# First block's attention queued behind the second chunk's chain, attention later in the first four periods, second layer three tiles behind the first

## The chip, the cores and the metric

The kernel runs on one core of one Trainium2 chip. The time is device microseconds (us) of one execution, and the median of several executions counts; lower is better. A core has five engines with a queue of their own each: TensorE (PE; its weight loads are shown as PEld), VectorE (DVE), ScalarE (ACT), GpSimd (POOL) and SyncE (SP, which here only issues DMA transfers). Each engine works through its own instructions in the order in which the built program has them.

## The reference

Two stages. The first is a complex gated linear attention over 4 batches, 8 heads, 768 tokens and head size 48; its output, seen as 3072 tokens of 384 channels, goes through eight dense expert networks (384 to 1024 to 384) that are weighted by a gate with eight rounds of row and column normalisation.

```python
for t in range(S):
    new_re = ar * S_re - ai * S_im
    new_im = ar * S_im + ai * S_re
    S_re, S_im = new_re + kv, new_im          # kv = k[t] v[t]^T
    y[:, :, t] = einsum('bhd,bhde->bhe', q[:, :, t], S_re)
...
P = np.exp(logits)                            # logits = x @ w_gate, less their maximum
for _ in range(8):
    P /= P.sum(1, keepdims=True) + 1e-09
    P /= P.sum(0, keepdims=True) + 1e-09
    P *= N / E
for e in range(E):
    out += P[:, e:e + 1] * (np.maximum(x @ w1[e], 0.0) @ w2[e])
```

## The kernel before, in words

The 3072 tokens are cut into 12 **blocks** of 256, and each block into two **chunks** of 128. There are two phases.

Phase 1 makes the attention and, on the way, experts 0 and 1. For each block there are three pieces of work:

- The **chain** (`elem`, `chain`, `scan`): the gates a of the block (tile z) are normalised, multiplied up along the chunk by a scan of complex products on DVE (`cmul`: tiles cm_a, cm_b, or a, b in block 0), then turned into keys divided by the products (tile kh, L393) and queries times the products (tile z again, L400). ACT makes squares and reciprocal roots between (L362 to L368 at the start, L381 to L386 at the end). The results go to DRAM (kd, qd) and come back in another layout (ks, qs) before PE can use them. Block 0 runs its two chunks as two chains, one after the other, so that the first can start early.
- The **attention** (`mix`), a generator with five steps for each chunk, ten for a block: keys (transposes ktp, L438) and first scores (sp, L452); state (U, L447) and the other keys; outputs (y, L469) and second scores; state; outputs, the new state on DVE (L490 to L501) and the block's x as a pair of a rounded part xh (ACT, L503) and a rest xl (DVE, L504). Between scores and outputs DVE masks the scores (L455). ACT copies the chunk's last gate product out of qs (rr and rn, L419 to L421).
- The **experts** (`experts`): 16 tiles for a block (two experts, eight slices of 128 of the 1024). A tile is a first layer (ph, nine matmuls L176 to L178), a relu in two forms on ACT (hh, L182; hf, L183), a rest on DVE (hl, L184), and a second layer (po, six matmuls L155 to L157), which is issued LAG tiles later.

PE's order is written out by hand. In **period** i PE runs the 16 tiles of block i-1, and from tile number LEAD on one step of block i's attention after each tile; steps that are left at the end of the period follow without a tile between them. With LEAD = 4 the ten steps stand behind tiles 4 to 13. Block 0's attention runs before any tile, between the preparations of four of expert 1's weight slices (`load_w`: cast on ACT L123, difference on PE L127 and L128, copy on ACT L129); the other four slices are loaded in halves in period 1, one half behind each of its first eight tiles (`load_late`, L137 to L142). The orders on DVE, ACT and SP are made by a scheduler from the program's dependences and its own estimates of time; `issue_after(x)` makes it put what follows behind x on x's engine, without a wait.

Phase 2a (`phase2a`) runs the last block's remaining 14 tiles in small groups (`more(k)`), between the steps of the check, the softmax and the first normalisation rounds (`rows` on DVE, `columns` with one PE product cp, L573). Phase 2b runs experts 2 to 7 with matrix products of fewer multiplications; the remaining rounds stand in its first steps.

Of the kernel before, what the change touches and what calls it, by code (L numbers as in the profile page):

```python
# [18 lines left out]
CH = 128  # L19
# [3 lines left out]
SK = 112  # L23
N1 = 8
RING = 12
LAG = 2
LEAD = 4
TR = 4
TB = 32
UN = 768  # L30
# [1 line left out]
NS = UN // SUB  # L32
SU = 2
ITERS = 8
GT = 16


# [16 lines left out]
class Net:  # L54
# [132 lines left out]
    def phase1(self, c1, ca):  # L187
        tc, nc = self.tc, self.nc
        PS = bass.MemoryType.PSUM
        self.hp = c1.enter_context(tc.tile_pool(name="hp1", bufs=3))  # L190
        wx = c1.enter_context(tc.tile_pool(name="wx", bufs=NF + N1 - RING))
        self.xp = c1.enter_context(tc.tile_pool(name="xp1", bufs=2))
        self.psB = c1.enter_context(tc.tile_pool(name="psB", bufs=2, space=PS))
        self.fix = ca.enter_context(tc.tile_pool(name="fix", bufs=1, side="right"))
        self.ain = ca.enter_context(tc.tile_pool(name="ain", bufs=2, side="right"))
        self.tmp = ca.enter_context(tc.tile_pool(name="tmp", bufs=2, side="right"))
        self.psS = ca.enter_context(tc.tile_pool(name="psS", bufs=2, space=PS))
        self.psY = ca.enter_context(tc.tile_pool(name="psY", bufs=1, space=PS))
# [12 lines left out]
        self.ist = 0  # L211
        self.rr = [fix.tile([SK, H], F32, name=f"rr{i}") for i in range(2)]
        self.rn = [fix.tile([SK, H], F32, name=f"rn{i}") for i in range(2)]
        self.sb = fix.tile([SK, H, D], F32, name="sb")
        for t in self.rr + [self.sb]:
            nc.gpsimd.memset(t, 0.0)
        self.xs, self.vt, self.kqd = {}, {}, {}
        ns = self.N // SUB
        self.moe = self.experts()
        next(self.moe)  # L220
        self.elem(0, True)
        for f in range(NF):
            self.load_w(0, f, wx)
        late = [(1, f, j) for f in range(RING - NF, NF) for j in range(2)]

        for i in range(ns):
            mix = self.mix(i)
            if i == 0:
                for n, _ in enumerate(mix):
                    if n % 2 == 0 and n < 2 * (RING - NF):  # L230
                        with tc.issue_after(self.kd0.ins), tc.issue_after(self.sq0.ins):
                            self.load_w(1, n // 2, wx)
                with tc.issue_after(self.gl.ins):
                    self.elem(1)
                continue
            lg = self.logits(i - 1)
            for n in range(2 * NF):
                self.moe.send((i - 1, n // NF, n % NF))
                if n in (1, 2):
                    next(lg)  # L240
                if late:
                    self.load_late(*late.pop(0), wx)
                if n >= LEAD:
                    next(mix, None)
            for _ in mix:
                pass
# [100 lines left out]
    def chain(self, i, ns_, zt, qk, alloc):  # L347
# [30 lines left out]
        for j in range(CH, ZW):  # L378
            nc.scalar.activation(cut(zt[:, :, :, j:j + 1]), z[:, :, :, CH - 1:CH], AF.Copy)
        sq, x, g0 = alloc("sq"), alloc("x"), alloc("g0")  # L380
        sq_ = nc.scalar.activation(sq, z, AF.Square)  # L381
        V.scalar_tensor_tensor(x, sq[:, 0], 1e-26, sq[:, 1], ALU.max, ALU.add)
        o = 2 * ns + i * NCT * NCH + n0 * NCT
        nc.scalar.activation(fl[:, o:o + G], x[:, :, CH - 1], AF.Copy)
        nc.scalar.activation(g0, x, AF.Abs_reciprocal_sqrt)
        nc.scalar.activation(g0, g0, AF.Square)  # L386
        V.tensor_tensor(x, x, g0, ALU.mult)
        self.gl = V.scalar_tensor_tensor(g0, x, -2.0, g0, ALU.add, ALU.mult)
        V.scalar_tensor_tensor(x, g0, -1.0, qk[:, 1], ALU.mult, ALU.mult)
# [1 line left out]
        kd, qd = self.kqd[i]  # L391
        for a in range(2):
            V.tensor_tensor(kh[:, a], x, z[:, a], ALU.mult)  # L393
            dma = nc.sync.dma_start(
                kd[a, :, ns_].rearrange("(c p) n t -> p c (n t)", c=NCT),
                kh[:, a].rearrange("p (c n) t -> p c (n t)", c=NCT))
        if i == 0 and n0 == 0:
            self.kd0, self.sq0 = dma, sq_
        for a in range(2):
            V.tensor_tensor(z[:, a], z[:, a], qk[:, 0], ALU.mult)  # L400
            nc.sync.dma_start(
                qd[a, :, ns_].rearrange("(c p) n t -> p c (n t)", c=NCT),
                zt[:, a].rearrange("p (c n) t -> p c n t", n=NCH)[:, :, ns_].rearrange("p c n t -> p c (n t)"))

    def mix(self, i):
        nc, tmp = self.nc, self.tmp
# [5 lines left out]
        for c in range(NCH):  # L412
            ib = (i * NCH + c) % 2
            qs, ks, rr, rn = self.qs[ib], self.ks[ib], self.rr[ib], self.rn[ib]
            for a in range(2):
                nc.sync.dma_start(ks[64 * a:64 * a + D], kd[a, :, c].rearrange("(h d) t -> d h t", d=D))
                nc.sync.dma_start(qs[64 * a:64 * a + D], qd[a, :, c, :CH + 1].rearrange("(h d) t -> d h t", d=D))
            R = qs[:, :, CH]
            nc.scalar.activation(rr[0:D], R[0:D], AF.Copy)  # L419
            nc.scalar.activation(rr[64:64 + D], R[0:D], AF.Copy)  # L420
            nc.scalar.activation(rn[0:D], R[64:64 + D], AF.Copy, scale=-1.0)  # L421
            first = (i % self.nsub == 0) and c == 0
            lastc = (i % self.nsub == self.nsub - 1) and c == NCH - 1
            S0, S1 = self.st[self.ist], self.st[1 - self.ist]
# [5 lines left out]
            def keys(g, i=i, c=c, ks=ks, kts=kts, lastc=lastc):  # L430
# [6 lines left out]
                for j in range(4):  # L437
                    nc.tensor.transpose(kt_p[:, j, :], ks[:, 4 * g + j, :], self.ident[:SK, :SK])  # L438
                kts[g] = tmp.tile([128, 4, SK], F32, tag="kt", name=f"kt{i}_{c}_{g}", bufs=2)
                nc.scalar.activation(kts[g], kt_p, AF.Copy)  # L440

            def state(g, c=c, U=U, kts=kts, lastc=lastc):
                if lastc:
# [34 lines left out]
            scores(1)  # L478
            yield
            state(1)  # L480
            yield
            outs(1)
            if not lastc:
# [163 lines left out]
    def phase2a(self, c2):  # L647
# [14 lines left out]
        def more(k):  # L662
            for _ in range(k):
                self.moe.send(todo.pop(0))

        for job in self.load_x(xa, 0, 0):
            job()
        more(2)
        self.check(xa, more)
        self.sinkhorn(xa, more)  # L670
        for k in range(ITERS // 2):
            self.rows()
            more(2)
# [8 lines left out]
    def phase2b(self, c2):  # L682
# [47 lines left out]

        V, A = nc.vector, nc.scalar
        jobs, free = [], [(pool, tag) for pool, tag in ((self.psC, "po0"), (self.psC, "po1"), (self.psC, "po2"), (psD, "po"), (psD, "po"))]
        it = ITERS // 2
        for n, st in enumerate(steps + [None]):
            prev = steps[n - 1] if n else None
            if st is None:
# [258 lines left out]
```

## Time and profile before

| | us |
|---|---|
| median of three runs | 1902.98 (1901.15 to 1905.99) |
| the profiled execution | 1904.32 |
| its span, first to last instruction | 1902.5 |
| PE busy in the span | 1784.5 (94%) |
| DVE busy | 1364.5 (72%) |
| ACT busy | 735.3 (39%) |
| end of phase 1's and 2a's tiles (last L157) | 726.0 |

The granted TensorE clock is a mean of 0.979 of full speed. A row of the timeline reads: start in us, duration in us, engine, line, operation, tile written <- tiles read, shapes, how many of them are merged in the row, and in square brackets how long the engine sat idle before it and whose result ended that. A row of the waits reads: engine, line and tile that waited, the releaser, then us in total, times, and the longest. A row of a table by stretches reads: the stretch, its length, and for PE, PEld, DVE, ACT and POOL the busy us with the number of instructions, then the granted clock, the DMA share and GB/s.

### The profile page before, as it was taken

How to read it: one execution, taken by the hardware profiler on the slowest of the kernel's cores; microseconds unless marked ns; L12 is line 12 of the kernel's file. 1: busy time of each engine (PE TensorE's matmuls, PEld its weight loads, DVE VectorE, ACT ScalarE, POOL GpSimd, SP SyncE). 2: the span in 40 equal slices, each digit the busy share in tenths (PEclk: the TensorE clock that was granted, in tenths of full speed). 3: DMA queues.
4: the chain of work that ended last, by engine and by line, in shares of the span. 5: the costliest groups of instructions: out<-in, count | busy, mean ns of one | idle time of the engine just before them, and what ended most of it. 6: DMA issues, size and time to landing. Idle time of an engine off the chain costs nothing.

```text
span 1902.5 us, 30283 instructions
## 1 busy us (share of the span) xinstructions
PE 1784.5 (94%) x12012; PEld 1730.6 (91%) x12012; DVE 1364.5 (72%) x3060; ACT 735.3 (39%) x1614; POOL 6.4 (0%) x15
## 2 busy tenths in 40 slices
PE   3749899999999999999999999999999999999998
PEld 2638888999899988999999999999999999999998
DVE  6678778888885367876767676777786767676754
ACT  5334444444444353333333333333342424242321
POOL 1000000000000000000000000000000000000000
PEclk8779999999999999999999999999999999999999
DMA  7455555444443242230101010123120101010100
GB/s 204 107 114 145 145 143 140 136 132 132 137 129 112 86 135 84 67 100 17 51 17 50 17 51 17 50 91 126 46 87 19 50 17 50 18 50 18 50 22 31
DMA packets 137782, 151.83 MB, mean 80 GB/s; under 512 B 7328, under 2 KB 117664, under 8 KB 137632
## 3 DMA queue, kind: packets, MB, share of 16 engines
q1 hardware_dynamic: 136832, 149.42, 27.0%
q8 instruction: 96, 1.57, 0.3%
q14 instruction: 54, 0.44, 0.1%
q10 hardware_dynamic: 800, 0.39, 0.1%
HBM read 107.17 MB, written 42.61 MB: 79 GB/s over the span
## 4 chain that ended last, share of the span: by engine, by line
PE 75%; DVE 11%; DMA 9%; ACT 3%; issue 2%; SPq 1%; DVEq 0%; ACTq 0%
PE po L720 10%; PE po L719 10%; PE po L718 10%; PE P L757 9%; PE P L758 9%; PE P L759 9%; DMA qs<-qd 4%; PE po L157 2%; PE po L155 2%; PE ph L177 2%; PE ph L178 2%; PE ph L176 2%; PE po L156 2%; PE sp L452 2%; DMA qd<-z 1%
## 5 line engine op out<-in xcount | busy, mean ns | idle before, releaser
L720 PE MATMUL po<-wc,hl 128*128 128x384 f32 x1152 | 386.0, 335 | 3.6 <-DVE hl L779 3.6
L719 PE MATMUL po<-wc,hh 128*128 128x384 f32 x1152 | 385.2, 334 | 0.0
L718 PE MATMUL po<-wc,hh 128*128 128x384 f32 x1152 | 385.2, 334 | 0.0
L778 ACT ACTIVATE hh<-c 128x384 fp32r<-128x384 f32 x384 | 201.0, 524 | 320.8 <-DVE c L767 319.2
L779 DVE SCALAR_TENSOR_TENSOR hl<-c,hh 128x384 fp32r<-128x384 f32 x384 | 211.9, 552 | 66.6 <-ACT hh L778 58.6
L720 PEld LDWEIGHTS po<-wc,hl 128*128 128x128 f32 x1152 | 216.6, 188 | 5.1 <-DVE hl L779 5.1
L718 PEld LDWEIGHTS po<-wc,hh 128*128 128x128 f32 x1152 | 216.5, 188 | 0.0
L719 PEld LDWEIGHTS po<-wc,hh 128*128 128x128 f32 x1152 | 216.5, 188 | 0.0
L772 ACT ACTIVATE s<-P 128x384 f32<-128x384 f32 x192 | 94.2, 491 | 276.3 <-PE P L759 276.1
L177 PE MATMUL ph<-xl,w 128*128 128x256 f32 x576 | 163.5, 284 | 2.1 <-DVE xl L504 2.1
L176 PE MATMUL ph<-xh,w 128*128 128x256 f32 x576 | 163.2, 283 | 0.6 <-ACT xh L503 0.6
L178 PE MATMUL ph<-xh,w 128*128 128x256 f32 x576 | 163.3, 283 | 0.0
L757 PE MATMUL P<-B,wa 128*128 128x384 f32 x480 | 160.7, 335 | 2.0 <-DVE c L767 1.4
L759 PE MATMUL P<-B,wa 128*128 128x384 f32 x480 | 160.4, 334 | 0.0
L758 PE MATMUL P<-B,wa 128*128 128x384 f32 x480 | 160.3, 334 | 0.0
L155 PE MATMUL po<-w,hh 128*128 128x384 f32 x384 | 142.5, 371 | 11.4 <-ACT hh L182 11.2
L182 ACT ACTIVATE hh<-ph 128x256 fp32r<-128x256 f32 x192 | 72.9, 380 | 204.8 <-PE ph L178 204.3
L157 PE MATMUL po<-w,hl 128*128 128x384 f32 x384 | 134.2, 349 | 13.7 <-DVE hl L184 12.5
L184 DVE TENSOR_TENSOR hl<-hf,hh 128x256 fp32r<-128x256 f32 x192 | 80.5, 419 | 78.2 <-ACT hf L183 77.5
L156 PE MATMUL po<-w,hh 128*128 128x384 f32 x384 | 130.5, 340 | 0.0
L767 DVE TENSOR_TENSOR c<-P,u 128x384 f32<-128x384 f32 x192 | 106.3, 554 | 31.8 <-PE P L759 30.3
L767 DVE TENSOR_TENSOR u<-u,s 128x384 f32<-128x384 f32 x96 | 53.4, 556 | 101.1 <-ACT s L772 100.9
(188 smaller groups left out, 3665.8 us busy)
## 6 DMA issues: line engine op xcount, KB each, us to landing
raw<-in_w_dram SPq DMA_DIRECT2D x48, 768.0 KB, 4.2
qs<-qd SPq DMA_DIRECT2D x48, 193.5 KB, 5.8
qk<-in_aqk_dram SPq DMA_DIRECT2D x12, 768.0 KB, 7.6
ks<-kd SPq DMA_DIRECT2D x48, 192.0 KB, 4.2
ye_d<-yst SPq DMA_DIRECT2D x48, 192.0 KB, 2.2
y<-ye_d SPq DMA_DIRECT2D x48, 192.0 KB, 2.4
qd<-z SPq DMA_DIRECT2D x22, 390.0 KB, 4.8
z<-in_aqk_dram SPq DMA_DIRECT2D x11, 768.0 KB, 8.8
```

The costliest lines, as they stand in the source:

```text
L155: nc.tensor.matmul(po[k], hh[:, s], w2h, start=f == 0, stop=False)
L176: nc.tensor.matmul(ph, w[:, 0, cs], xh[:, ct, :], start=(ct == 0), stop=False)
L177: nc.tensor.matmul(ph, w[:, 0, cs], xl[:, ct, :], start=False, stop=False)
L178: nc.tensor.matmul(ph, w[:, 1, cs], xh[:, ct, :], start=False, stop=(ct == NCT - 1))
L718: nc.tensor.matmul(po[k], hh[:, s], w2[:, 0, i], start=first, stop=False)
L719: nc.tensor.matmul(po[k], hh[:, s], w2[:, 1, i], start=False, stop=False)
L720: nc.tensor.matmul(po[k], hl[:, s], w2[:, 0, i], start=False, stop=last)
L757: nc.tensor.matmul(ps, t[:, 0, k], x[:, 0], start=first, stop=False)
L758: nc.tensor.matmul(ps, t[:, 0, k], x[:, 1], start=False, stop=False)
L759: nc.tensor.matmul(ps, t[:, 1, k], x[:, 0], start=False, stop=last)
L778: A.activation(hh, c, AF.Relu)
L779: V.scalar_tensor_tensor(hl, c, 0.0, hh.bitcast(F32), ALU.max, ALU.subtract)
```

## The change

```diff
-LAG = 2
-LEAD = 4
+LAG = 3
+LEAD = {1: 11, 2: 10, 3: 8, 4: 6}
...
+HEAD = 3
...
-        self.hp = c1.enter_context(tc.tile_pool(name="hp1", bufs=3))
+        self.hp = c1.enter_context(tc.tile_pool(name="hp1", bufs=LAG + 1))
...
             if i == 0:
-                for n, _ in enumerate(mix):
+                n = 0
+                while True:
+                    with tc.issue_after(self.act0.ins), tc.issue_after(self.dve0.ins):
+                        if next(mix, self) is self:
+                            break
                     if n % 2 == 0 and n < 2 * (RING - NF):
-                        with tc.issue_after(self.kd0.ins), tc.issue_after(self.sq0.ins):
+                        with tc.issue_after(self.act0.ins), tc.issue_after(self.q0.ins):
                             self.load_w(1, n // 2, wx)
+                    n += 1
...
-                if n >= LEAD:
+                if n >= LEAD.get(i, 4):
                     next(mix, None)
...
-        nc.scalar.activation(g0, g0, AF.Square)
+        act = nc.scalar.activation(g0, g0, AF.Square)
...
-            V.tensor_tensor(z[:, a], z[:, a], qk[:, 0], ALU.mult)
+            dve = V.tensor_tensor(z[:, a], z[:, a], qk[:, 0], ALU.mult)
...
+        if i == 0:
+            self.act0, self.dve0 = act, dve
...
-                nc.sync.dma_start(qs[64 * a:64 * a + D], qd[a, :, c, :CH + 1].rearrange("(h d) t -> d h t", d=D))
+                dma = nc.sync.dma_start(qs[64 * a:64 * a + D], qd[a, :, c, :CH + 1].rearrange("(h d) t -> d h t", d=D))
+            if i == 0 and c == 0:
+                self.q0 = dma
             R = qs[:, :, CH]
-            nc.scalar.activation(rr[0:D], R[0:D], AF.Copy)
-            nc.scalar.activation(rr[64:64 + D], R[0:D], AF.Copy)
-            nc.scalar.activation(rn[0:D], R[64:64 + D], AF.Copy, scale=-1.0)
...
-                nc.scalar.activation(kts[g], kt_p, AF.Copy)
+                self.kt = nc.scalar.activation(kts[g], kt_p, AF.Copy)
...
             state(1)
+            if not lastc:
+                with self.tc.issue_after(self.kt.ins):
+                    nc.scalar.activation(rr[0:D], R[0:D], AF.Copy)
+                    nc.scalar.activation(rr[64:64 + D], R[0:D], AF.Copy)
+                    nc.scalar.activation(rn[0:D], R[64:64 + D], AF.Copy, scale=-1.0)
             yield
...
-        more(2)
+        more(1)
         self.check(xa, more)
         self.sinkhorn(xa, more)
-        for k in range(ITERS // 2):
+        for k in range(HEAD):
             self.rows()
-            more(2)
+            more(3)
             self.columns(self.psK.tile([128, E], F32, tag="po", name=f"cp{k}"))
...
-        it = ITERS // 2
+        it = HEAD
```

In words: (1) On ACT and DVE, all that block 0's attention puts there stands behind the last square and the last product of the second chunk's chain, and the loads of expert 1's first four slices stand behind that square on ACT and behind chunk 0's queries (qs) on SP. (2) The attention of blocks 1 to 4 begins behind tiles 11, 10, 8 and 6 of its period in place of tile 4; so five, four, two and none of its ten steps are left for the period's end. (3) A second layer is issued three tiles behind its first layer, with one more buffer for hh and hl. (4) The copies of the chunk's last gate product (rr, rn) are made in the chunk's fourth step, behind its second copy of keys (kt) on ACT, and not at all for the last chunk of a batch. (5) In phase 2a three normalisation rounds stand in place of four, with three tiles between rows and columns in place of two and one tile less before the check; the fourth round moves into phase 2b's first steps, where five rounds stand then.

Where it moves instructions, at the places that the prediction speaks of:

ACT at the start, in the order before, from the square that ends the first chunk's chain (L386 above it is not shown) to the one that begins the end of the second's; in these names w1_0 to w1_3 are expert 1's slices, kt0_0_0 the keys of block 0's chunk 0, and kh0 <- z0 the square L381 of chunk 1.

```order
L123 ACTIVATE w1_0_498<-wr1_0_499 128x768
L379 ACTIVATE z0_199<-z0_199 128x6 x2
L440 ACTIVATE kt0_0_0_490<-ktp0_0_0_485 128x448
L123 ACTIVATE w1_1_535<-wr1_1_536 128x768
L123 ACTIVATE w1_2_566<-wr1_2_567 128x768
L419 ACTIVATE rr0_191<-qs0_175 48x8
L420 ACTIVATE rr0_191<-qs0_175 48x8
L381 ACTIVATE kh0_210<-z0_199 128x6x128
```

The same place now:

```order
L385 ACTIVATE z0_199<-z0_199 128x6 x2
L387 ACTIVATE kh0_210<-z0_199 128x6x128
L390 ACTIVATE fl_91<-x0_211 128x3
L391 ACTIVATE zz0_213<-x0_211 128x384
L392 ACTIVATE zz0_213<-zz0_213 128x384
L445 ACTIVATE kt0_0_0_487<-ktp0_0_0_482 128x448
L124 ACTIVATE w1_0_495<-wr1_0_496 128x768
L124 ACTIVATE w1_1_532<-wr1_1_533 128x768
```

The square of chunk 1 (kh0 <- z0) and the two operations behind it stood behind the copies of keys, gates and weights, which wait for transfers or for PE; now they stand right behind z0's copy, and the keys and weight casts come after them.

PE at block 1's keys, before (ph0_0_4 is expert 0's tile 4 of block 0, wd1_6_0 a late half slice, ktp1_0_0 and sp1_0_0 block 1's keys and scores):

```order
L178 MATMUL ph0_0_4_924<-xh0_474,w0_4_426 128x256
L140 MATMUL wd1_6_0_944<-wr1_6_0_941,ident_70 128x384
L141 MATMUL wd1_6_0_944<-w1_6_940,nident_72 128x384
L438 MATMUL ktp1_0_0_959<-ident_70,ks0_177 128x112 x4
L452 MATMUL sp1_0_0_966<-qs0_175,ks0_177 128x128 x4
L155 MATMUL po0_0_0_853<-w0_3_414,hh0_0_3_905 128x384
L156 MATMUL po0_0_0_853<-w0_3_414,hh0_0_3_905 128x384
L157 MATMUL po0_0_0_853<-w0_3_414,hl0_0_3_906 128x384
```

And now (ph1_0_3 is tile 11):

```order
L179 MATMUL ph1_0_3_1110<-xh0_474,w1_3_608 128x256
L443 MATMUL ktp1_0_0_1134<-ident_70,ks0_177 128x112 x4
L457 MATMUL sp1_0_0_1141<-qs0_175,ks0_177 128x128 x4
L156 MATMUL po1_0_0_1102<-w1_1_532,hh1_0_1_1068 128x384
L157 MATMUL po1_0_0_1102<-w1_1_532,hh1_0_1_1068 128x384
L158 MATMUL po1_0_0_1102<-w1_1_532,hl1_0_1_1069 128x384
L156 MATMUL po1_0_1_1106<-w1_1_532,hh1_0_1_1068 128x384
L157 MATMUL po1_0_1_1106<-w1_1_532,hh1_0_1_1068 128x384
```

The keys stood behind tile 4 and stand behind tile 11 now; the second layer that follows belongs to tile 3 before, the one in front of it, and to tile 9 now, two in front of the tile just issued. The second chunk of block 1 (five steps, from ktp1_1_0 on) stands behind tile 15, and behind its last outputs come one second layer and the first tile of block 1.

DVE at block 1's second chunk, behind its second masked scores, before (z3 and the cm tiles are block 3's chain, tm1_1, sa1_1 and sb the new state, xl1 the rest that the next period's tiles read):

```order
L372 TENSOR_TENSOR z3_2037<-z3_2037,x3_2046 128x6x128 x2
L490 TENSOR_TENSOR tm1_1_1337<-st1_188,U1_1_1180 112x384
L184 TENSOR_TENSOR hl1_0_4_1290<-hf1_0_4_1291,hh1_0_4_1289 128x256
L265 TENSOR_TENSOR cm_a_2060<-z3_2037 128x12x32
L265 TENSOR_TENSOR cm_b_2061<-z3_2037 128x12x32
L497 TENSOR_TENSOR sa1_1_1339<-tm1_1_1337,rr1_192 112x384
L499 TENSOR_TENSOR sb_195<-tm1_1_1337,qs1_176 48x384
L500 TENSOR_TENSOR sb_195<-tm1_1_1337,rn1_194 48x384
L184 TENSOR_TENSOR hl1_0_5_1316<-hf1_0_5_1317,hh1_0_5_1315 128x256
L269 TENSOR_TENSOR z3_2037<-cm_a_2060,cm_b_2061 128x6x32
L270 TENSOR_TENSOR z3_2037<-cm_a_2060,cm_b_2061 128x6x32
L504 TENSOR_TENSOR xl1_949<-y1_1_1179,xh1_948 128x3x128
```

And now, from the product in front of these scores on (x2, g02 and x3, y03 belong to the chains of blocks 2 and 3):

```order
L369 SCALAR_TENSOR_TENSOR x3_2037<-sq3_2036 128x768
L460 COPY_PREDICATED sc1_180<-mask_74,sp1_1_1_1346 128x512
L393 TENSOR_TENSOR x2_1488<-x2_1488,g02_1489 128x768
L500 TENSOR_TENSOR tm1_1_1375<-st1_188,U1_1_1305 112x384
L394 SCALAR_TENSOR_TENSOR g02_1489<-x2_1488,g02_1489 128x768
L372 TENSOR_TENSOR x3_2037<-x3_2037,zz3_2039 128x768
L507 TENSOR_TENSOR sa1_1_1377<-tm1_1_1375,rr1_192 112x384
L509 TENSOR_TENSOR sb_195<-tm1_1_1375,qs1_176 48x384
L510 TENSOR_TENSOR sb_195<-tm1_1_1375,rn1_194 48x384
L395 SCALAR_TENSOR_TENSOR x2_1488<-g02_1489,qk2_1387 128x768
L373 SCALAR_TENSOR_TENSOR y03_2038<-x3_2037,y03_2038 128x768
L514 TENSOR_TENSOR xl1_1127<-y1_1_1304,xh1_1126 128x3x128
```

Before, DVE's rests hl of tiles 12 and 13 stand between scores and xl1, since the experts go on meanwhile; now there is none, x3 (which waits for a square on ACT) stands in front of the scores, and nine products stand between the scores and xl1.

More of the change, by code (lines that the diff above doesn't have):

```diff
@@ L380, in chain @@
         sq, x, g0 = alloc("sq"), alloc("x"), alloc("g0")
-        sq_ = nc.scalar.activation(sq, z, AF.Square)
+        nc.scalar.activation(sq, z, AF.Square)
         V.scalar_tensor_tensor(x, sq[:, 0], 1e-26, sq[:, 1], ALU.max, ALU.add)
@@ L393, in chain @@
             V.tensor_tensor(kh[:, a], x, z[:, a], ALU.mult)
-            dma = nc.sync.dma_start(
+            nc.sync.dma_start(
                 kd[a, :, ns_].rearrange("(c p) n t -> p c (n t)", c=NCT),
                 kh[:, a].rearrange("p (c n) t -> p c (n t)", c=NCT))
-        if i == 0 and n0 == 0:
-            self.kd0, self.sq0 = dma, sq_
         for a in range(2):
-            V.tensor_tensor(z[:, a], z[:, a], qk[:, 0], ALU.mult)
+            dve = V.tensor_tensor(z[:, a], z[:, a], qk[:, 0], ALU.mult)
             nc.sync.dma_start(
```

## Prediction, blind

> **What bounds the kernel now.** I first read the table of busy time by stretches, cut where the stages change (first tiles at 81, block 1's scores at 128, end of phase 2a at 726).
>
> ```profile
> 0.00:81.00 81.00, 41.99 (x248) 30.01 (x248) 52.73 (x170) 39.27 (x84) 6.36 (x15) 0.79 0.58 160
> 81.00:128.00 47.00, 17.84 (x95) 15.07 (x96) 36.41 (x91) 17.10 (x41) 0.00 (x0) 0.71 0.59 140
> 128.00:726.00 598.00, 567.50 (x5038) 535.85 (x5037) 452.24 (x1086) 266.76 (x701) 0.00 (x0) 0.99 0.46 129
> 726.00:800.00 74.00, 71.61 (x402) 70.07 (x401) 58.05 (x138) 26.55 (x53) 0.00 (x0) 0.98 0.20 59
> 800.00:1902.00 1102.00, 1085.52 (x6235) 1079.62 (x6234) 765.03 (x1577) 385.66 (x737) 0.00 (x0) 1.00 0.14 46
> ```
>
> Length less PE busy is PE's idle time: 39.0 us before the first tiles, 29.2 in the next stretch, 30.5 in the rest of phases 1 and 2a, 2.4 and 16.5 in phase 2b. The busy times add up to 1784 of 1902 us, so PE's order is the bound from 81 on, and what can be won is idle time before 726, 98.7 us. DVE, at 452 of 598, is next. The change touches nothing behind 800. The waits of PE name who ends its idle times:
>
> ```profile
> PE ktp L438 <- DMA ks<-kd: 36.5, 3, 18.9
> PE sp L452 <- DMA qs<-qd: 16.7, 3, 7.9
> PE po L157 <- DVE hl L184: 12.5, 17, 2.1
> ...
> PE po L155 <- ACT hh L182: 11.2, 7, 4.1
> ...
> PE cp L573 <- DVE cs L569: 4.4, 3, 2.0
> ```
>
> The first two hold one big pair: block 1's keys and scores wait 18.9 + 7.9 = 26.8 us for kd and qd to come back through DRAM. The next two, 23.7 us, are second layers that wait for their relu or its rest; the last is phase 2a.
>
> **Part 1, block 0's attention behind the second chain.** ACT's row of the square L381 and DVE's rows around it show who waits, and PE's two rows what follows:
>
> ```profile
> 48.22 0.85 ACT L381 ACTIVATE kh<-z 128x768 f32<-128x768 f32 x1
> ```
>
> On DVE:
>
> ```profile
> 41.13 0.25 DVE L270 TENSOR_TENSOR z<-a,b 128x93 f32<-128x93 f32 x1
> 49.10 0.56 DVE L382 SCALAR_TENSOR_TENSOR x<-kh 128x384 f32<-128x384 f32 x1 [7.71 <-ACT kh L381]
> ```
>
> On PE:
>
> ```profile
> 68.72 2.08 PE L452 MATMUL sp<-qs,ks 112*128 112x128 f32 x8 [5.58 <-DMA qs<-qd]
> ...
> 83.74 0.39 PE L177 MATMUL ph<-xl,w 128*128 128x256 f32 x1 [2.05 <-DVE xl L504]
> ```
>
> DVE ends chunk 1's scan at 41.4; the square that the chain needs next starts at 48.2, since on ACT it stands behind casts and gate copies; DVE sits idle for 7.7. Now it is next on ACT, so x (L382) starts at about 42.3 in place of 49.1, 6.8 earlier; a weight cast and a mask copy that stood among the next steps move behind them, some tenths more. The transfers of chunk 1 follow the chain, then its scores (68.7) and the first tile (83.7). The four weight loads now stand behind qs on SP, but PE needs them only between the steps of this attention. I take **-7.0**; ends 0 (if the later loads fall on chunk 1's transfers) and -7.7.
>
> **Part 2, block 1's keys behind tile 11.** PE's rows give the pace of a tile and the wait:
>
> ```profile
> 92.52 0.91 PE L140 MATMUL wd<-wr,ident 128*128 128x384 f32 x2
> ...
> 93.44 0.34 PE L155 MATMUL po<-w,hh 128*128 128x384 f32 x1
> ...
> 94.49 0.28 PE L176 MATMUL ph<-xh,w 128*128 128x256 f32 x1
> ...
> 98.83 0.63 PE L141 MATMUL wd<-w,nident 128*128 128x384 f32 x1
> 118.37 0.98 PE L438 MATMUL ktp<-ident,ks 112*128 112x112 f32 x4 [18.90 <-DMA ks<-kd]
> 127.24 2.05 PE L452 MATMUL sp<-qs,ks 112*128 112x128 f32 x8 [7.90 <-DMA qs<-qd]
> ...
> 182.26 0.28 PE L176 MATMUL ph<-xh,w 128*128 128x256 f32 x1
> ...
> 184.37 0.28 PE L176 MATMUL ph<-xh,w 128*128 128x256 f32 x1
> ```
>
> A tile with its second layer takes 2.11 (182.26 to 184.37), a late half slice 0.92 (92.52 to 93.44), a second layer alone 1.05 (93.44 to 94.49). PE comes to the keys at 99.5 now. In the changed kernel seven more tiles and three more late halves come first, one second layer fewer: 99.5 - 7.0 + 7 x 2.11 + 3 x 0.92 - 1.05 = 109.0. The data come by block 1's chain on DVE: 127.2 - 7.0, and another 1.7 earlier, because one complex product of the scan (by the rows of part 3 two operations of 0.58 and two half as long) now stands in front of block 0's last masked scores, where DVE idles: 118.5. The wait is 118.5 - 109.0 - 0.4 for the keys = 9.1 in place of 26.8: **-17.7**. Ends: no wait, -26.8; a chain that gains nothing from part 1, wait 18, -9.
>
> **Part 3, what is late next: the steps without a tile between.** After tile 15 of the period, block 1 has its whole second chunk left, block 2 four steps, block 3 two; block 4's last step stands behind tile 15. There PE waits for DVE and ACT, and the next period's first tile waits for xl. In the rows before, block 0's second chunk shows such a tail: from its first scores at 68.7 to the first tile at 83.7 is 15.0 us, with weight preparations between. For block 1 I add up DVE's queue as the order has it:
>
> ```profile
> 143.33 0.55 DVE L490 TENSOR_TENSOR tm<-st,U 112x384 f32<-112x384 f32 x1 [0.43 <-PE U L447]
> 143.91 0.56 DVE L497 TENSOR_TENSOR sa<-tm,rr 112x384 f32<-112x384 f32 x1
> ...
> 149.52 0.95 DVE L366 TENSOR_TENSOR x<-x,zz 128x768 f32<-128x768 f32 x1
> 150.39 0.95 DVE L389 SCALAR_TENSOR_TENSOR x<-g,qk 128x768 f32<-128x768 f32 x1
> ...
> 151.59 0.72 DVE L455 COPY_PREDICATED sc<-mask,sp 128x512 f32<-128x512 uint8 x1
> ...
> 153.07 1.82 DVE L393 TENSOR_TENSOR kh<-x,z 128x768 f32<-128x768 f32 x2
> ```
>
> And ACT's squares and root:
>
> ```profile
> 96.91 1.49 ACT L381 ACTIVATE sq<-z 128x1536 f32<-128x1536 f32 x1
> ...
> 99.90 0.84 ACT L385 ACTIVATE g<-x 128x768 f32<-128x768 f32 x1
> 100.64 1.48 ACT L362 ACTIVATE sq<-z 128x1536 f32<-128x1536 f32 x1
> ```
>
> A 128x768 product takes 0.87 from start to start (149.52 to 150.39), a 128x384 one 0.58 (143.33 to 143.91). Between the masked scores of the second chunk's two halves stand x2, which waits for a square of 1.5, and x3, which waits for the root (0.84) behind x2 and a second square: 1.5 + 0.9 + 0.8 + 1.5 + 0.9 = 5.6. Behind the second masked scores come five products of the first kind and four of the second, 6.7, then xl, 0.6. With the two masks (0.7 each) that is 14.3, and DVE comes to the first mask some 4 us after PE, since it has the rest of block 2's scan and the first chunk's state to do on the way. PE has 6 us of its own steps in there: idle 12. Block 2: 4.7 between its masks (z3, x4, two of z4, a pair of cm), 3.5 from there to xl, and about 3.5 by which the first mask is late, less 3.5 of PE's work: 8. Block 3: 1.5, block 4: 0.5. Together **+22**. Ends: +8, were each tail only the 2.05 that the first tile waits for xl at 83.74; +38, if the first two cost block 0's 15.0 and the others 5 and 3.
>
> **Part 4, gate copies and LAG.**
>
> ACT's rows of block 2's gate copies, then PE's of the same place and of a shorter wait:
>
> ```profile
> 221.76 0.21 ACT L419 ACTIVATE rr<-qs 48x8 f32<-48x8 f32 x1 [5.87 <-DMA qs<-qd]
> ...
> 224.25 0.21 ACT L421 ACTIVATE rn<-qs 48x8 f32<-48x8 f32 x1 [1.66 <-DMA qs<-qd]
> 224.36 0.36 ACT L182 ACTIVATE hh<-ph 128x256 fp32r<-128x256 f32 x1
> ```
>
> On PE:
>
> ```profile
> 224.78 0.69 PE L155 MATMUL po<-w,hh 128*128 128x384 f32 x1 [4.13 <-ACT hh L182]
> ...
> 226.31 0.52 PE L156 MATMUL po<-w,hh 128*128 128x384 f32 x1
> 226.63 0.52 PE L157 MATMUL po<-w,hl 128*128 128x384 f32 x1
> ...
> 230.79 0.29 PE L176 MATMUL ph<-xh,w 128*128 128x256 f32 x1
> ...
> 484.76 0.44 PE L157 MATMUL po<-w,hl 128*128 128x384 f32 x1 [2.13 <-DVE hl L184]
> ```
>
> ACT sits for 5.9 and 1.7 us with rr and rn at its head, waiting for qs, and the relu hh behind them is late: PE waits 4.1. Behind kt they find qs landed, because kt needs keys that PE transposes after the scores. That takes most of the 11.2 us of L155. The rests hl (12.5 us, 17 waits, the longest 2.1) are late because DVE is in a long product; a third tile gives them another 2.11 us each, as much as the longest. I take **-21** of 23.7; ends -11 (the copies alone) and -24. After the 4.1 us wait the clock is slow: 224.78 to 230.79 holds twelve second-layer and nine first-layer matmuls, 3.2 us at the pace of the rows above, in 6.0; so it costs 2.8 more. The waits that go save that two or three times, the tails bring as many: 0.
>
> **Part 5, phase 2a.** cp waits 4.4 us for the rows of normalisation; with three tiles (6.3 us) between, I take **-4** (ends 0 and -4.4). The round that moves is hidden in phase 2b, where PE is busy 1085.5 of 1102; its few DVE operations would have to wait 2 us of PE to be seen.
>
> **The sum**, against the profiled execution: 1904.3 - 7.0 - 17.7 + 22 - 21 - 4 = 1876.6. That execution lies 1.3 over the median of the runs shown, so I say **1876**.
>
> **The rivals.** (a) *DVE's chain is the bound of the first periods.* For: before, kh of block 2 (153.07) starts 25.8 behind block 1's scores (127.24); in the changed order one complex product more, three short ones (about 1 each) and the second chunk's mask and state (about 4) stand in between, so it comes 34.5 behind 118.5, at 153 again, and DVE has won nothing by then. Against: DVE is busy 76% from 128 to 726, so it catches up. If it holds to block 4, parts 2 to 4 count half: 1904.3 - 7 - 8.9 + 11 - 10.5 - 4 = 1885. Chance 0.13. (b) *LAG only moves the wait*: hl is in time, and the first layer waits for ACT to empty one of its two buffers; then part 4 gives 11: 1887. 0.10. (c) *Slow clock behind every gap.* Six gaps of 3 to 9 us (block 1's data, three in its tail, two in block 2's) against three before: three times 2.8 more, 1885. For: 224.78; against: 484.76, where a wait of 2.1 us leaves the next matmuls fast, so the shorter ones may be free. 0.10. The Trainium skill, TensorE: Matmul & The Clock Gate, section "HAM oscillation — how this bites in real kernels", asks for no idle gap over about 3.4 us; the two rows agree with it, and by it the tails' gaps lie at the edge. (d) *Slower:* the first layer waits for ACT in every tile, because with LAG 3 no second layer in between shows that hf is done; over 12 x 16 tiles 0.144 us each takes back the 27.7, and 0.3 us gives 1876.6 + 57.6 = 1934. Against: ACT is busy 267 of 598 us, and has 3.15 us for a relu pair. 0.04. (e) *The tails are cheap*, 8 to 12 us: 1863 to 1867. 0.15. That the keys would not move cannot be, as PE's order is fixed in the program.
>
> **How the numbers follow.** The forecast (1868 to 1884) has 0.48, (e) 0.15, (a) to (c) 0.33, (d) 0.04. The range takes in (a) to (c), and (e) with part 2 at its better end: **1860 to 1892**. About 0.3%, 5.7 us, can be told from no change here. Faster by more than that: all but (d) and the outer part of (a) and (b), 0.91; within it 0.05; slower 0.04.
>
> **What would show it.** Right: L382 of chunk 1 starts near 42 on DVE; sp of block 1 starts near 118 after a wait of 9; a wait of some 5 us in front of the first tile of block 1, for xl; no hh wait over 1 us in periods 2 to 10; cp without a wait. Wrong: a first layer that waits for ACT; block 2's or 3's scores waiting for qs; last L157 later than 705.

## The result and the profile after

The changed kernel took **1854.79 us** (median of four runs, 1853.66 to 1856.9) against 1903.86 for the kernel before in the same session: a ratio of 0.9744, 95% interval 0.9727 to 0.9761, or 49 us less. The forecast was 1876, its range ended at 1860. The sign was right and the size was not: about 28 us were forecast, 49 came.

The table by stretches of the changed kernel, cut at the same times as that of before (columns as there):

```profile
0.00:81.00 81.00, 46.08 (x272) 34.16 (x273) 62.23 (x208) 40.95 (x90) 6.36 (x15) 0.83 0.63 178
81.00:128.00 47.00, 40.82 (x292) 38.22 (x291) 34.26 (x84) 24.45 (x62) 0.00 (x0) 0.93 0.54 131
128.00:726.00 598.00, 579.45 (x5082) 558.03 (x5082) 477.20 (x1141) 273.26 (x693) 0.00 (x0) 0.98 0.47 131
```

PE's idle time in the second stretch falls from 29.2 us to 6.2, which is where block 1's keys and scores had waited. The waits of PE in the changed kernel (lines of the weight and expert functions are one higher than before, those of the attention five, or ten from the new state on, those of phase 2 ten) show what has gone and what is new:

```profile
PE sp L457 <- DMA qs<-qd: 12.6, 3, 6.2
...
PE ktp L443 <- DMA ks<-kd: 12.4, 1, 12.4
PE y L474 <- DVE sc L460: 10.3, 6, 4.2
PE ph L178 <- DVE xl L514: 6.2, 4, 2.6
...
PE cp L583 <- DVE cs L579: 0.5, 1, 0.5
```

The second layers wait for hh no more (11.2 us before) nor for hl (12.5); in the keys' row 12.4 of 36.5 us are left, all of them at block 0. New is y, which waits for masked scores, and the waits for xl have grown from 2.1 us to 6.2: the steps without a tile between. But these rows do not add up to 49 us. All idle time of PE in the span falls from 1902.5 - 1784.5 = 118.0 us to 76.6, by 41.4. The other 7.7 us are in PE's *busy* time, which the page gives as

```profile
PE 1776.8 (96%) x12012; PEld 1733.4 (94%) x12012; DVE 1361.7 (73%) x3060; ACT 734.6 (40%) x1602; POOL 6.4 (0%) x15
```

against 1784.5 for the same 12012 matmuls. The prediction counted waits only, and called the matmuls' own pace even.

So I cut each kernel at the routing product lp of a period (in its second tile), where the work behind the cut is alike, and read length, PE busy and clock of each part. Here a period has the number of the block whose tiles it runs, one less than in the text ahead of the prediction. Of the kernel before, periods 1, 2 to 3 and 4 to 10:

```profile
177.70:231.90 54.20, 49.41 (x437) 47.06 (x435) 42.30 (x105) 23.19 (x61) 0.00 (x0) 0.94 0.50 128
231.90:336.10 104.20, 98.22 (x886) 92.49 (x884) 85.90 (x210) 47.86 (x126) 0.00 (x0) 1.00 0.50 133
336.10:681.80 345.70, 334.99 (x3057) 316.40 (x3055) 248.12 (x578) 149.24 (x399) 0.00 (x0) 1.00 0.43 125
```

And of the changed kernel, the same three with period 0 ahead:

```profile
80.50:153.30 72.80, 61.51 (x476) 56.44 (x474) 57.42 (x125) 35.82 (x83) 0.00 (x0) 0.86 0.44 115
153.30:209.50 56.20, 49.85 (x437) 47.69 (x435) 50.42 (x123) 22.61 (x57) 0.00 (x0) 0.91 0.67 161
209.50:308.30 98.80, 96.49 (x886) 92.78 (x884) 87.25 (x216) 48.14 (x126) 0.00 (x0) 1.00 0.59 152
308.30:636.50 328.20, 328.20 (x3058) 317.00 (x3055) 246.92 (x574) 151.02 (x397) 0.00 (x0) 1.00 0.45 133
```

Periods 4 to 10 have no idle time left. They became 17.5 us shorter where the rows of before held 10.7 us of idle time; the other 6.8 us went out of the matmuls, at a granted clock of 1.00 in both. Phase 2b is the same (1176.5 and 1176.7 us). Which of the five parts of the change did this is what the runs had to tell.

### The profile page after: what moved, and what is told of

The parts are those of the page before. It is cut to its first block, busy times and chain, and to the rows that moved or that the text cites. A ratio compares the mean times of both kernels' runs of the same rounds, so it can differ in the third digit from the quotient of the medians.

```text
span 1853.4 us, 30293 instructions
## 1 busy us (share of the span) xinstructions
PE 1776.8 (96%) x12012; PEld 1733.4 (94%) x12012; DVE 1361.7 (73%) x3060; ACT 734.6 (40%) x1602; POOL 6.4 (0%) x15
## 3 DMA queue, kind: packets, MB, share of 16 engines
q1 hardware_dynamic: 136832, 149.42, 27.7%
## 4 chain that ended last, share of the span: by engine, by line
PE 83%; DVE 9%; DMA 5%; ACT 1%; issue 1%; SPq 1%; DVEq 0%
PE po L730 10%; PE po L729 10%; PE po L728 10%; PE P L767 9%; PE P L768 9%; PE P L769 9%; PE po L156 3%; PE ph L178 3%; PE ph L179 3%; PE ph L177 3%; PE po L158 3%; PE po L157 3%; PE sp L457 2%; PE y L474 2%; PE U L452 1%; DMA raw<-in_w_dram 1%
## 5 line engine op out<-in xcount | busy, mean ns | idle before, releaser
L178 PEld LDWEIGHTS ph<-xl,w 128*128 128x128 f32 x576 | 110.1, 191 | 7.3 <-DVE xl L514 7.3
```

Of the source, the lines that this page charges most:

```text
L178: nc.tensor.matmul(ph, w[:, 0, cs], xl[:, ct, :], start=False, stop=False)
```

## Experiments

A ratio stands to the kernel before, as it ran in the same session, with its 95% interval; a difference in us between two kernels is that of their ratios times 1903.

### What made the second layers late

**Copies put back.** The changed kernel with the gate copies where they were:

```diff
             R = qs[:, :, CH]
+            nc.scalar.activation(rr[0:D], R[0:D], AF.Copy)
+            nc.scalar.activation(rr[64:64 + D], R[0:D], AF.Copy)
+            nc.scalar.activation(rn[0:D], R[64:64 + D], AF.Copy, scale=-1.0)
...
-            if not lastc:
-                with self.tc.issue_after(self.kt.ins):
-                    ...
```

> The changed kernel with the gate copies rr and rn back ahead of the keys. Theory S: with LAG 3 a relu may be 2 us later, so of the two long hh waits (3.3 and 4.1 us in the kernel before) 1 to 2 us each come back, and the slow clock behind them: 1856 to 1862. Rival C (the copies are what made the second layers late, all along): hh and hl waits come back in most periods, 1868 or more.

1884.87 us, ratio 0.9921 (0.9891 to 0.9950): 34 us of the gain are gone, far over what theory S said. Rival C has the time and not its sign: with LAG 3 no wait of a second layer for hh or hl comes back in phase 1. PE waits elsewhere for what ACT delivers late, in periods 0 to 10 for hf (5.5 us in the first layer), for kt (5.2) and for the outputs that ACT copies out (yst, 5.9), and 8.5 us for xl. ACT's waits in the kernel before show where ACT itself stands:

```profile
ACT rr L419 <- DMA qs<-qd: 66.7, 20, 8.1
...
ACT rn L421 <- DMA qs<-qd: 21.0, 16, 4.4
```

For 87.7 us ACT stands with a copy of 48x8 numbers (0.2 us of work) at its head, waiting for the queries to come back from DRAM. The prediction used two of these 36 waits, those that delay a relu at once.

**Copies alone, LAG alone**, each from the kernel before (the first with the lines above the other way round):

```diff
-LAG = 2
+LAG = 3
...
-name="hp1", bufs=3
+name="hp1", bufs=LAG + 1
```

> The kernel before with nothing but the gate copies moved behind the keys. Theory A (formed from the run with the copies put back: a copy that waits for qs at the head of ACT's queue, 87.7 us in 36 waits in the kernel before, makes the relu and its rest late, and with them the hh and the hl waits of the second layers): nearly all of the 40 us that the accounts give to those waits, 1862 to 1872, and hl waits under 4 us. Rival P (the copies give the hh rows alone, the hl rows belong to LAG): 11.2 us of rows and about half as much behind them, 1884 to 1890, with hl waits of some 12 us left.

1868.15 us, ratio 0.9814 (0.9797 to 0.9832): theory A. The hh waits are gone, ACT's waits name rr and rn no more, and of the hl waits 3.6 us are left, with LAG still 2:

```profile
PE po L157 <- DVE hl L184: 3.6, 5, 1.4
```

Periods 1, 2 to 3 and 4 to 10 of this kernel:

```profile
170.40:218.10 47.70, 46.33 (x437) 44.41 (x435) 42.41 (x107) 22.60 (x57) 0.00 (x0) 1.00 0.58 150
218.10:314.10 96.00, 96.00 (x886) 92.81 (x884) 84.81 (x203) 47.70 (x124) 0.00 (x0) 1.00 0.61 159
314.10:644.20 330.10, 329.29 (x3057) 316.78 (x3055) 249.53 (x587) 150.57 (x397) 0.00 (x0) 1.00 0.45 131
```

Against the rows of before the three lose 30.3 us, 19.3 of idle time and 11.0 of busy time. The copies alone are worth more than the whole forecast.

> The kernel before with nothing but LAG 3. Theory A: the copies still hold ACT for up to 8 us at a time, more than one tile of 2.1 us can hide, and the rows saved are the shorter ones: 1888 to 1902. Rival P (the hl waits, the longest 2.1 us, are what LAG hides): 12.5 us of rows and some 8 behind them go, 1880 to 1885, with no hl waits left.

1890.15 us, ratio 0.9951 (0.9932 to 0.9970), theory A's time. The hl rows fall from 12.5 to 0.2 us, as rival P had it, but a row takes their place, the prediction's rival (b):

```profile
PE ph L176 <- ACT hf L183: 10.1, 8, 2.3
```

The first layer waits for ACT to empty its buffers. The wait changed its name and its place; ACT is what is late.

**Is it ACT on the chip, or the order?** With the copies moved, the build also lays out DVE's order anew, and in the kernel before hl often stood 2 to 4 us behind hf on DVE. So I took the copies off ACT and left every other order as it was (in the two traces PE, DVE and ACT run the same instructions in the same order, but for the 72 copies):

```diff
-            nc.scalar.activation(rr[0:D], R[0:D], AF.Copy)
-            nc.scalar.activation(rr[64:64 + D], R[0:D], AF.Copy)
-            nc.scalar.activation(rn[0:D], R[64:64 + D], AF.Copy, scale=-1.0)
+            nc.gpsimd.tensor_scalar(rr[0:D], R[0:D], 1.0, None, ALU.mult)
+            nc.gpsimd.tensor_scalar(rr[64:64 + D], R[0:D], 1.0, None, ALU.mult)
+            nc.gpsimd.tensor_scalar(rn[0:D], R[64:64 + D], -1.0, None, ALU.mult)
```

> The kernel before with the gate copies on GpSimd, at their old place in the program; the built orders on PE, DVE and SP and what is left on ACT are those of the kernel before, row for row. So the chip's own effect of copies that hold ACT goes, and what the copies did to the other engines' orders stays. In the kernel before, 15 of the 17 hl waits have hf within 2 us of its tile and hl 2 to 4 us behind hf on DVE. Theory O (two ways: the hh waits come from ACT held on the chip, the hl waits from DVE's order, which was laid out with the copies on ACT): the hh rows and what follows them go, 12 to 20 us, and 10 us or more of hl waits stay, 1882 to 1891. Theory A (one way: everything late comes from ACT held on the chip, DVE's lateness too): as with the copies moved, 1865 to 1872, hl waits under 5 us.

1868.61 us, ratio 0.9824 (0.9809 to 0.9839), the same as with the copies moved, no hh waits and 4.0 us of hl waits: theory A, and theory O falls. GpSimd now waits in ACT's place, and the waits of PE name GpSimd nowhere:

```profile
PE po L157 <- DVE hl L184: 4.0, 6, 1.1
```

```profile
POOL rr L419 <- DMA qs<-qd: 326.9, 16, 38.8
```

How a wait of ACT becomes a wait of PE for *DVE* can be followed in the kernel before. On ACT, then on DVE, then on PE:

```profile
467.18 0.21 ACT L419 ACTIVATE rr<-qs 48x8 f32<-48x8 f32 x1 [4.60 <-DMA qs<-qd]
...
468.17 0.36 ACT L183 ACTIVATE hf<-ph 128x256 f32<-128x256 f32 x1
```

```profile
468.57 0.42 DVE L184 TENSOR_TENSOR hl<-hf,hh 128x256 fp32r<-128x256 f32 x1 [2.93 <-ACT hf L183]
...
484.29 0.42 DVE L184 TENSOR_TENSOR hl<-hf,hh 128x256 fp32r<-128x256 f32 x1
```

```profile
482.30 0.34 PE L156 MATMUL po<-w,hh 128*128 128x384 f32 x1
484.76 0.44 PE L157 MATMUL po<-w,hl 128*128 128x384 f32 x1 [2.13 <-DVE hl L184]
485.04 0.34 PE L155 MATMUL po<-w,hh 128*128 128x384 f32 x1
```

The copy holds ACT for 4.60 us, so hf is late, so DVE sits for 2.93 us with hl at its head. DVE has no idle time behind that to make it up, and four hl later, 16 us on, PE waits 2.13 us; it names DVE, and the hf of that tile had ended at 480.48. With the copies on GpSimd the same two hl, in the same order, and the same matmul of PE stand at

```profile
437.93 0.42 DVE L184 TENSOR_TENSOR hl<-hf,hh 128x256 fp32r<-128x256 f32 x1
...
454.02 0.42 DVE L184 TENSOR_TENSOR hl<-hf,hh 128x256 fp32r<-128x256 f32 x1
```

```profile
454.49 0.44 PE L157 MATMUL po<-w,hl 128*128 128x384 f32 x1 [1.07 <-DVE hl L184]
```

The first has no wait in front, and PE's wait for the second is 1.07 us in place of 2.13; the other 1.07 us are there without the copies too. The Trainium skill, Perfetto Trace Analysis, section "Tensor Engine Instruction (MATMUL, LD_WEIGHTS)", says that ACT's and DVE's execution queues are strictly first in, first out; these rows agree.

### LEAD and LAG once the copies are out of the way

From the changed kernel, `LEAD = {}` (4 everywhere), `LAG = 2`, and both; from the kernel before, the table of LEAD alone.

> The changed kernel with LEAD 4 in all periods. The accounts of both traces give the table 21.4 us less of wait for block 1's data and 24.6 us more for steps without a tile between. Theory S: the two cancel, so LEAD 4 gives 1850 to 1856, with a wait of some 23 us for block 1's keys and scores in place of 6.2 and no wait for xl behind the period. Rival W (waiting at block 1's data with nothing else to do also makes DVE late for blocks 2 to 4, since its masked scores stand in front of the next block's scan): 1865 to 1875, with waits for qs or sc in periods 1 to 3.

1848.77 us, ratio 0.9724 (0.9704 to 0.9745), 4 us below the changed kernel, with an interval that overlaps its own, and a little under theory S's range. Its periods 0, 1 and 2 to 3:

```profile
78.50:158.70 80.20, 55.80 (x475) 51.58 (x474) 67.06 (x148) 35.76 (x85) 0.00 (x0) 0.83 0.55 133
158.70:205.10 46.40, 46.16 (x436) 44.50 (x435) 41.37 (x103) 22.69 (x57) 0.00 (x0) 1.00 0.56 151
205.10:301.10 96.00, 96.00 (x886) 92.82 (x885) 85.17 (x205) 48.01 (x124) 0.00 (x0) 1.00 0.60 160
```

The four periods take 222.6 us in place of 227.8. The table takes 18.2 us off block 1's wait (24.4 to 6.2) and gives back 23.4: 13.6 as waits for masked scores and xl, the rest as slower matmuls (PE is busy for 61.5 and 49.9 us in periods 0 and 1, where with LEAD 4 it is for 55.8 and 46.2). Rival W falls: with nothing to do while block 1's data come, DVE is not late for what follows.

> The changed kernel with LAG 2 again. Measured so far: changed 1855, before 1904. Theory S (the second layers' waits cost the rows of 23.7 us and another 16 us of slower matmuls behind each, and LAG 3 is what takes them away): the hl waits come back, 17 of them or more, 12.5 us in their rows and some 8 behind them, and a few us of hh: 1872 to 1882. Rival D (the later attention and the moved copies leave DVE and ACT free in time, LAG matters little): under 5 us, 1855 to 1860, with fewer than five waits of the second layer in its rows.

1847.95 us, ratio 0.9715 (0.9695 to 0.9735): outside both ranges, on the good side, some 5 us below the changed kernel (the intervals overlap a little). Only 3.2 us of hl waits came back, and period 0 lasts 68.3 us in place of 72.8, though it has a second layer more in it: 2.1 us less of idle time and 2.4 of busy time. Why was not followed up.

> The changed kernel with both LAG 2 and LEAD 4, so that only the copies, block 0's queueing and phase 2a are changed. Apart, LAG 2 gave 1848 and LEAD 4 gave 1849 where the changed kernel gave 1855. Theory A (LAG and LEAD cost at separate places: LAG 3 makes the tails longer by a second layer at slow clock, LEAD makes the tails): the second gain is partly the first one, 1843 to 1849. Rival L (without later attention DVE is busier in each period, and LAG 3 is needed): hl waits come back as in the kernel before, 1855 to 1865.

1850.19 us, ratio 0.9722 (0.9705 to 0.9740): as with either alone, 1 us above theory A's range and far from rival L, with 4.4 us of hl waits. Without LAG 3 and without the table the rest of the change gives all of the gain. What the table costs depends on LAG: with LAG 2 the four periods take 223.2 us with it and 225.3 without, 2 us less in place of 5 more; block 1's wait falls by 18.3 us (24.1 to 5.8), and some 16 come back.

> The kernel before with nothing but the table of LEAD. Theory A (the table changes only what PE does while block 1's data come; its tails cost about as much as it saves; in the changed kernel it cost 6 us): 1900 to 1912. Rival Q (it needs the freed ACT to cost so little; with the copies waiting in the tails, each tail gets longer): 1915 to 1930.

1898.76 us, ratio 0.9983 (0.9973 to 0.9993), 3 us faster, 1 us below theory A's range and far from rival Q: with the copies in place, too, what the table saves at block 1 it gives back behind.

### The start and phase 2a

The changed kernel with the old lines for block 0 (`issue_after` on kd0 and sq0 for the loads alone), and with the old lines for phase 2a:

```diff
-HEAD = 3
+HEAD = 4
...
-        more(1)
+        more(2)
...
-            more(3)
+            more(2)
```

> The changed kernel with block 0's attention and expert 1's first loads queued as before. The start to the first tile took 8.6 us less in the changed kernel, and block 1's scores follow the same chain. Theory S: everything behind moves by the same 8 us, 1863 (1861 to 1865). Rival H (the start is hidden by the chain of DVE that follows, which bounds the first periods): under 4 us, 1856 to 1859.

1862.94 us, ratio 0.9798 (0.9778 to 0.9819), 10 us above the changed kernel (8 by the medians): theory S in sum, though not as it said. The start up to the first lp is only 3.3 us longer (83.8 and 80.5); 2.0 more stand in period 1, 0.8 in phase 2a and 1.8 in phase 2b.

> The changed kernel with phase 2a as before: four rounds of normalisation in it, two tiles between them. Theory: the cp waits of 4.4 us come back and nothing else, 1858 to 1860 (changed kernel 1855). Rival: the round that was moved into phase 2b had cost there what it saved here, 1854 to 1856.

1862.73 us, ratio 0.9800 (0.9785 to 0.9815), 11 us above the changed kernel (8 by the medians), about twice what the theory's waits give. From the last lp to the last second layer it lasts 48.5 us in place of 40.2 (44.2 in the kernel before), with cp waits of 6.1 us, not 4.4, and slower matmuls behind them (clock 0.93 for 1.00). The run with LAG 3 alone shows the same: that part lasts 49.4 us there, with a clock of 0.90, while the four kernels with LAG 2 and the old phase 2a (the one before, copies alone, copies on GpSimd, table alone) have 44.2 to 46.1. So it is with LAG 3 that the old phase 2a costs more; why its cp waits then grow (the longest from 2.0 to 3.1 us) was not tried.

### A version that is faster than both

If the tails cost as much as the wait they save, the best LEAD is the largest that leaves almost none: `LEAD = {1: 6}` puts block 1's last step behind tile 15, `{1: 8}` leaves two steps.

> The changed kernel with the table cut to one entry, LEAD 6 for block 1 and 4 for the others. With LEAD 4 everywhere (1849) PE waited 24.4 us for block 1's data and had no tail; the tenth step stood behind tile 13. Theory T (the wait is for data whose time doesn't depend on LEAD, so each tile put ahead of the keys saves its 2.1 us and the late half slice's 0.9 until the tenth step has no tile behind it): 6 us less, 1841 to 1845. Rival V (what bounds the first periods is DVE's chain from block 1's masked scores on, which waits for the same data, so tiles moved ahead of it are missed behind it): 1847 to 1851, with the 6 us coming back as waits for sc, xl or qs in periods 1 and 2.

> The same with LEAD 8 for block 1: two tiles more ahead of the keys, two steps of block 1's attention behind the period's last tile. Theory T: 6 us less wait than with LEAD 6, and a tail of two steps (a mask, the state, the third product and xl, some 5 to 7 us at slow clock): equal to LEAD 6 within 3 us, 1840 to 1846. Rival V: the tail comes on top of what is missed behind, 1849 to 1855.

> LEAD 6 for block 1 and LAG 2. Alone with LEAD 4, LAG 2 and 3 gave 1850 and 1849. Theory A (once the copies are out of the way LAG decides nothing): within 3 us of LEAD 6 with LAG 3. Rival L (with steps packed closer LAG 3 is needed): 4 us or more above it, in hl waits.

1846.33, 1845.70 and 1848.26 us; ratios 0.9706 (0.9693 to 0.9719), 0.9701 (0.9687 to 0.9715) and 0.9721 (0.9707 to 0.9734). The first two beat the changed kernel by 7 to 8 us; the third's interval overlaps that of the changed kernel. None of the three is clear of LEAD 4 everywhere (0.9704 to 0.9745). LEAD 6 did take 7.5 us off block 1's wait against LEAD 4 (24.4 to 16.9), but 2.6 came back as a wait for xl and some 2 as busy time in the same period, and the start was 2.1 longer in that execution, so its time lies between theory T and rival V; the runs don't part them. LEAD 8 stands at theory T's value. LAG decides nothing here either.

## Why the forecast was too small, step by step

**Where the bound is.** Right: PE's idle time ahead of 726, and phase 2b untouched. Not seen: PE also loses time that no wait row holds.

**Part 1, the start: -7.0.** Right in sum. The square's reader L382 (now L388) starts at 42.23 (forecast 42.3), and the part up to the first lp is 7.8 us shorter (88.3 to 80.5). Not all of it is the queueing of block 0: with the copies alone that part was 2.4 shorter (85.9), with the old queueing 3.3 longer.

**Part 2, block 1's wait: -17.7.** Right in kind, 3 us small (26.8 to 6.2 is 20.6, of which the table of LEAD has 18.2). In the changed kernel:

```profile
108.01 0.55 PE L443 MATMUL ktp<-ident,ks 112*128 112x112 f32 x4
114.74 2.05 PE L457 MATMUL sp<-qs,ks 112*128 112x128 f32 x8 [6.18 <-DMA qs<-qd]
```

Keys at 108.0 (forecast 109.0), scores at 114.7 (118.5), a wait of 6.2 (9.1). Why the data came 3.8 us earlier than forecast was not tried.

**Part 3, the tails: +22.** Right in sum, 23.4 by the run with LEAD 4. They are 13.6 us of waits and some 10 us of slower matmuls, where the forecast put all of it into waits. Slow clock behind gaps, rival (c), is seen here: behind a wait of only 2.4 us in block 1's tail the scores take twice the time that they took 6 us before (the granted clock is 0.50 from 136.1 to 144, and 1.00 from 126 to 133.5),

```profile
131.58 1.07 PE L457 MATMUL sp<-qs,ks 112*128 112x128 f32 x8
...
136.15 0.65 PE L474 MATMUL y<-sc,v 128*32 128x128 f32 x8 [2.36 <-DVE sc L460]
...
138.02 2.08 PE L457 MATMUL sp<-qs,ks 112*128 112x128 f32 x8
...
148.60 0.38 PE L178 MATMUL ph<-xl,w 128*128 128x256 f32 x1 [2.60 <-DVE xl L514]
```

But the slow matmuls do not set the length of this tail. In the run with the old phase 2a, which has the same instructions in the same order up to there, the same wait (2.35 us at 136.13) is followed by a clock of 1.00 from 139.5 on, and the first tile of block 1 starts at the same time, behind a longer wait:

```profile
148.58 0.58 PE L178 MATMUL ph<-xl,w 128*128 128x256 f32 x1 [4.52 <-DVE xl L514]
```

DVE sets it: from its second masked scores to xl it takes 6.5 us in both (forecast 6.7), in both after a wait of 2.48 us for ACT's square. So the mechanism was right here, and how the 23.4 us divide into waits and slow matmuls is a matter of the execution.

With part 2, LEAD was forecast to cost 4.3 us in all and cost 5.2; with LAG 2 the same table cost nothing.

**Part 4, gate copies and LAG: -21. This is the step that failed.** From the kernel before to the one with the copies alone, periods 0 to 10 became 35.2 us shorter, and LAG 3 adds some 2 us in periods 4 to 10. Two statements were wrong. The first: "The rests hl (12.5 us, 17 waits, the longest 2.1) are late because DVE is in a long product". DVE was in a long product, but late for it because ACT had been held by a copy; the copies alone, with LAG 2, took 8.9 of the 12.5 us. The view that says so is ACT's waits, 87.7 us at rr and rn, of which the prediction used two rows, with ACT busy only 39% of the span. The second: "The waits that go save that two or three times, the tails bring as many: 0". That set slow matmuls behind the long waits that go (two or three times 2.8 us) against as many in the tails. Periods 0 to 10 lost 22.7 us of idle time to the copies, close to the forecast's -21, and 12.5 us of busy time; the tails' slow matmuls stand within the 23.4 us of part 3, so nothing stood against these 12.5, which the sum had at 0. In periods 4 to 10 the clock is 1.00 all through; there the loss sits at the edges of each wait. Of the rows at 484.76 above: matmuls of a second layer start 0.17 to 0.18 us apart, but this one starts 2.46 behind the one before it, where the wait row says 2.13, and its successor follows in 0.28. So this wait costs 0.27 us more than its row, and the same working gives 0.26 or 0.27 at every wait for hl that the rows of periods 1 to 10 list; the 15 waits of any kind that periods 4 to 10 list would then give 4.1 of their 6.8 us. Some such losses show in no row of the waits:

```profile
272.47 0.45 PE L155 MATMUL po<-w,hh 128*128 128x384 f32 x1 [1.54 <-ACT hh L182]
272.76 0.34 PE L156 MATMUL po<-w,hh 128*128 128x384 f32 x1
273.20 0.45 PE L157 MATMUL po<-w,hl 128*128 128x384 f32 x1
```

From 272.76 to 273.20 the matmul hh is drawn as busy for 0.34 us and no wait is listed behind it, yet 0.27 us are lost before hl. The Trainium skill's page Perfetto Trace Analysis, in the section named above, says that the end of a TensorE instruction is worked out from its size, not observed; the rows fit that: the same 3057 matmuls are "busy" for 335.0, 329.3 or 328.2 us at the same clock.

**Part 5, phase 2a: -4.** The part from the last lp on is 4.0 us shorter (44.2 to 40.2), cp's wait fell from 4.4 to 0.5. Its worth to the changed kernel is twice that or more, by the run with the old lines, since with LAG 3 the old lines cost more.

**The rivals.** (a), DVE's chain as the bound, fell with the run with LEAD 4. (b), LAG that only moves the wait, is what LAG does while the copies stand in the way, and not after. (c) is seen in the tails, where it adds nothing to the length of block 1's. (d), a first layer that waits for ACT, has no row in the changed kernel. (e), cheap tails, fell.

**The sum.** Up to the last second layer the forecast was 27.7 us and 49.3 came. Of the 21.6 that lack, 14.2 are the copies (35.2 for 21), 1.9 LAG 3 in periods 4 to 10 on top of them, and 0.8 the start, less 0.9 at LEAD. The other 5.6 us stand in periods 0 to 3 between the kernel with the copies alone (228.2 us) and the changed one with LEAD 4 (222.6): 2.4 of them at block 1's data, 1.2 in period 1's waits, 1.1 a second layer that LAG 3 moves behind, the rest not assigned.

## What to carry to other kernels

Read the waits of *every* engine that works through its queue in order, also of one that is busy 39% of the time: a tiny instruction that waits for a transfer at its head held all that was queued behind it here, and what PE showed of it later bore another engine's name. Put such an instruction behind one that needs the same data to have landed, or on an engine for which nobody waits. And price a wait that goes at its row plus the matmuls around it: with the same instructions, compare PE's busy time too.

## What the runs showed of the hardware that was not expected

A wait of PE for hl cost 0.26 to 0.27 us beyond what its row says, with the clock granted in full. Slow matmuls follow shorter gaps than rival (c) reckoned with: behind 6.2 us at 114.74 the pace is back by 119.6 (U in 0.89 us), but behind 2.36 us at 136.15 it stays at half to two thirds up to the next gap, at 146. The length of a wait alone does not say which comes: behind 2.35 us at the same place the clock was back at 139.5 in another execution, and behind dense work a wait of 2.15 us was followed by a clock of 0.50 (table of LEAD alone, at 168.59), one of 2.13 by 1.00 (kernel before, at 484.76). And GpSimd made the 72 copies of 48x8 at no cost that the time shows (1868.61 us, and 1868.15 with the copies moved on ACT).
